# Sliding-window attention and a softplus feed-forward network: a fourth G buffer, two third differences in place, and the order of all steps rewritten

## The chip, the cores and the metric

The kernel runs on one core of one Trainium2 chip. Its time is the device time of one execution in microseconds (us); the figure for the kernel before is the median of three runs. Besides those runs there is one profiled execution, taken by the hardware profiler, with a time of its own. In profile rows PE is TensorE (PEld its weight loads), DVE is VectorE, ACT is ScalarE, POOL is GpSimd and SP is SyncE. POOL issues the loads, SP the DMA transposes and the stores.

## What is computed

The input is q, k, v of 4 batches, 8 heads, 768 positions and 64 columns, and two weight matrices, w_in (512 x 2048) and w_out (2048 x 512). Each position attends to the 8 first positions of its batch and to the 96 last ones up to itself, with a bias by distance whose slope depends on the head. The attention rows, 3072 tokens of 512 numbers, go through a feed-forward network with a softplus between its two products.

```python
rel = pos[:, None] - pos[None, :]
is_global = pos[None, :] < n_global                 # 8
is_local = (rel >= 0) & (rel < n_local)             # 96
dist = np.where(is_global & ~is_local, n_local, np.abs(rel))
scores = q @ k.T / sqrt(D) - slopes * dist          # else -1e9
a = softmax(scores)
x = (a @ v).transpose(0, 2, 1, 3).reshape(3072, 512)
h = x @ w_in
g = np.maximum(h, 0.0) + np.log1p(np.exp(-np.abs(h)))
return g @ w_out
```

## The kernel before

The tokens are cut into 24 blocks of 128 (six for each batch) for the attention, and into 12 chunks of 256 (two blocks each) for the network. A chunk's result of the softplus, with 2048 rows in 16 pieces of 128 x 256, is the tile G.

The program is a list of 1139 steps, the string ORDER (line 748). A step is a kind, one or two indices, and at the end for some kinds a digit that says which engine does it (0 DVE, 1 ACT; for the small copies gk and gv, 2 is POOL). Each engine carries out its instructions in the order of this list, so that the list alone sets every engine's order and that of the DMA queues. An instruction waits for the data that it reads and for the readers of the memory that it overwrites; everything behind it on its engine waits with it. The kinds:

- `lq`, `lk`, `lv` load q, k or v of a block, `wi` and `wo` parts of the weights (L103, L109, L114). All are issued by POOL, one after another. The rings for q and k hold six blocks in three tiles of a pair each, the ring for v seven. In the profile `k_t` stands for any tile of K's ring; in the order below `k_t2_83` is the tile of blocks 16 and 17, among others, and `k_t0_81` that of block 19.
- `t`, `tQ`, `tK` transpose q and k of the first blocks on PE, and `qc`, `kc` copy them to QT and KT. From block 8 on, `d` transposes q and k by DMA, issued by SP (L270, L271).
- `gk` and `gv` copy the eight global keys or values of the batch into a block's tiles (L312, L316). The copy of values goes into the tile of the block before, once that has been read for its own product.
- `s`, `ss` are the scores (L325), whose matmuls use half the array's rows; `ab`, `ac` add the bias (DVE, L385 and L394); `e` is the Exp (ACT, L405), which writes the weights Pb; `p` is the value product (PE, L421), half a block at a time; `nm` divides by the sum (DVE, L436 and L439) and writes the attention rows xsf. For the first blocks the bias is put into PSUM by a matmul instead (`z`, L351).
- `x` transposes attention rows on PE (L454) and `xc` copies them (L461) into XT; in later blocks `y` does it by DMA from SP.
- `f`, `fe`, `lp`, `o`, `os` are the plain network of the first chunks (L475 to L640).
- From chunk 2 on the first product is made by seven smaller products of a Strassen type: `ht` differences of x (DVE, L553), `h` the products (PE, L582), `hc` copies of one accumulator (ACT or DVE, L592, L595), `hv` sums of two (DVE, L607; the operand is called p_ps), `he` Exp (ACT, L612), `hl` the logarithm into G (ACT, L616). They use sums of quarters of w_in, made once by `hw` (DVE).
- From chunk 1 on the second product is made in the same manner: `gs` sums of G (DVE, L668), `m` the products (PE, L698), `ec` and `ev` evictions (L727 on ACT or DVE, L737 on DVE), `st` the stores (L711). They use differences of parts of w_out, made once by `wd` (DVE, L653).
- `g` is a gate (POOL, L746): a copy of one element of G, by which POOL waits there until ACT has written that part of G, so that the loads behind it do not start sooner.

The accumulators take turns in three banks of PSUM by the string BANKS (line 206); the scores and value products have banks of their own. G has three buffers.

```python
ffn = ctx.enter_context(tc.tile_pool(name="ffn", bufs=3))             # G
w_dif = {i: const.tile([P, NU, CT], F16, name=f"w_dif{i}") for i in (1, 2, 3, 4)}
def gv(n, by=0):
    if n % BPB >= 2:
        engine_copy(by)(v_t[n - 1][0:NG], v_t[first_of(n)][0:NG])
def gate(s):
    c, u = divmod(s, NU)
    nc.gpsimd.tensor_copy(gate_t[:], G[c][0:1, 2 * u + 1, 0:1])
for name in ORDER.split():
    kind = name.rstrip("0123456789.")
    KINDS[kind](*(int(i) for i in name[len(kind) :].split(".")))
```

The functions that the change touches:

Of the kernel before, what the change touches and what calls it, by code (L numbers as in the profile page):

```python
# [13 lines left out]
F16 = mybir.dt.float16  # L14
# [6 lines left out]
def kernel(  # L21
# [19 lines left out]
    CT = 2 * P  # L41
# [23 lines left out]
    ffn = ctx.enter_context(tc.tile_pool(name="ffn", bufs=3))  # L65
# [19 lines left out]
    w_dif = {i: const.tile([P, NU, CT], F16, name=f"w_dif{i}") for i in (1, 2, 3, 4)}  # L85
# [111 lines left out]
    def bias_part(half, part):  # L197
# [8 lines left out]
        "01201220102102102102012010010211021221212022020121202201001202012121011020020112"  # L206
        "022021102002111020202121010212020101"
# [285 lines left out]
    def plus(c, w):  # L493
# [146 lines left out]
    def w_half(i, j, part):  # L640
        return w_out_c[2 * i + part][:, :, CT * j : CT * j + CT]

    def w_dif_part(i, part, by=0):

        rows = slice(4 * part, 4 * part + 4)
        t = {n: w_dif[n][:, rows, :] for n in w_dif}
        a, b = {
            1: (w_half(0, 1, part), w_half(0, 0, part)),
            2: (w_half(1, 1, part), t[1]),
            3: (w_half(1, 1, part), w_half(0, 1, part)),  # L650
            4: (w_half(1, 0, part), t[2]),
        }[i]
        sum_by(by)(t[i], a, b, ALU.subtract)  # L653
# [5 lines left out]
    def g_sum(c, i, by=0):  # L659
# [21 lines left out]
        7: lambda c: (SM[c, 3], lambda k: w_dif[3][:, k, :]),  # L681
# [61 lines left out]
    def gate(s):  # L743
# [5 lines left out]
        lq1 bb0.1 w18 lk1 cq0 ck0 tq0 z0.0 z0.1 lq2 lk2 bb1.1 tk0 bb1.0 s0.1 lv0 t1 s0.0 lv1  # L749
        kc1.0 e0.1 lk4 z1.1 bb0.0 qc1.0 s1.1 e0.0 tQ2 e1.1 z1.0 s1.0 z2.1 tK2 lv2 gv19 p0.1 e1.0  # L750
        gk2.1 p0.0 qc2.0 lq4 lv3 kc2.1 nm0.1 nm0.0 wi1 z2.0 wi3 s2.0 s2.1 x0 lk5 qc3.1 kc3.0
        p1.0 gk3.2 p1.1 e2.0 nm1.0 z3.0 lq5 e2.1 s3.0 gv2.2 wi0 lv4 p2.0 wi2 p2.1 wi4 xc0.1
        nm1.1 z3.1 s3.1 e3.0 nm2.0 gv3.0 nm2.1 x1 t4 x2 e3.1 wo0 xc1.0 qc4.1 gk4.1 p3.0 p3.1
        kc4.1 nm3.0 nm3.1 f1 s4.0 lv5 xc2.1 wi6 fe1 x3 xc3.1 f3 f9 fe3 ab4.0 fe9 s4.1 wo1 t5
        ab4.1 qc5.0 wo2 f11 kc5.0 gk5.0 e4.0 f0 gv4.1 f8 wo3 e4.1 fe0 fe11 p4.0 nm4.0 lp0 s5.0
        fe8 f2 p4.1 ab5.0 fe2 nm4.1 f10 s5.1 gv5.1 f5 lk6 lq6 fe10 e5.0 lk7 lp1 x4 f4 ab5.1
        xc4.0 hw1.0 e5.1 lq7 wd1.0 f12 o0 p5.0 fe12 fe4 lp4 f13 fe13 o4 lq8 hw2.0 nm5.0 p5.1
        hw3.1 fe5 nm5.1 lp5 f14 hw4.0 fe14 lv6 hw1.1 lk9 f7 lp2 f6 x5 lk8 lq9 lv7 xc5.1 fe7 o1
        fe6 o5 lp3 f15 lq10 h2.1.0 fe15 hc2.1.0.1 o2 hw2.1 ht2.1 ht2.3 lp6 lp7 wd1.1 lk10 h2.5.0
        h2.2.0 gs1.3 hc2.5.0.1 hw3.0 wd3.0 wd2.0 ht2.2 wd2.1 ht2.4 wd4.1 o6 h2.6.0 d8 o7  # L760
        he2.11.0 wd3.1 t6 os0.1.1 hv2.6.0 kc6.1 h2.3.0 o3 gs1.1 hw4.1 qc6.1 gs1.2 he2.12.0
        os0.0.1 ss6 ab6.0 h2.7.0 ac6.1 t7 e6.0 kc7.1 hv2.7.0 lq14 d9 ac6.0 hl2.0.0 m1.1.0 st0.0
        qc7.0 p6.0 ec1.1.0 e6.1 h2.4.0 nm6.0 ss7 gk8.2 he2.22.0 he2.21.0 lv8 ac7.0 h2.1.1
        hc2.1.1.1 p6.1 ab7.0 m1.6 ac7.1 d10 ec1.6.1 lk11 e7.0 h2.5.1 wd4.0 h2.2.1 nm6.1 h2.6.1
        hc2.5.1.1 m1.2.1 g7 p7.0 hv2.6.1 he2.11.1 nm7.0 x6 e7.1 xc6.1 hl2.1.0 ev1.2 h2.7.1
        h2.3.1 hv2.7.1 lq11 p7.1 ss8 g15 nm7.1 ab8.0 he2.12.1 m1.7 ac8.0 x7 gk9.2 he2.22.1 ac8.1
        ec1.7.1 h2.4.1 xc7.1 ht3.1 m1.4 gs1.4 ss9 e8.0 ec1.4.0 lq13 h3.1.0 gv8.2 p8.0 he2.21.1
        e8.1 hc3.1.0.1 m1.5.0 ac9.0 nm8.0 lv10 h3.5.0 h3.2.0 ht3.3 ht3.2 lv9 lq12 hl2.1.1 h3.6.0
        ev1.5 m1.3 p8.1 hc3.5.0.1 lv11 d11 ab9.0 he3.11.0 hl2.0.1 h3.1.1 hv3.6.0 h3.7.0 h3.3.0
        ht3.4 ev1.3 nm8.1 st1.0 e9.0 hv3.7.0 he3.12.0 gs2.1 gv9.2 ac9.1 y8 m2.1.0 hc3.1.1.1  # L770
        h3.4.0 p9.0 h3.2.1 ec2.1.0 gk10.1 gs2.2 nm9.0 he3.21.0 e9.1 gs2.3 g21 st0.1 he3.11.1
        h3.6.1 h3.5.1 lk12 hc3.5.1.1 p9.1 hl3.0.0 nm9.1 hv3.6.1 ss10 m2.6 y9 gv10.2 ab10.0
        h3.3.1 he3.22.0 h3.7.1 gk11.2 ec2.6.1 ac10.0 m2.7 lq17 hv3.7.1 h4.1.0 he3.12.1 ac10.1
        lk15 e10.0 hl3.0.1 ec2.7.1 p10.0 nm10.0 lq16 h3.4.1 ht4.1 ss11 he3.21.1 m2.4 lk13 ac11.1
        e10.1 ac11.0 d12 ht4.2 ec2.4.1 ht4.3 h4.5.0 hc4.1.0.1 g27 hc4.5.0.1 ab11.0 lk14 m2.2.1
        h4.6.0 hl3.1.0 hv4.6.0 p10.1 e11.0 d13 h4.2.0 m2.5.0 h4.7.0 nm10.1 g23 st1.1 y10 gv11.2
        p11.0 he4.11.0 gs2.4 ev2.5 ev2.2 nm11.0 h4.3.0 e11.1 g13 m2.3 ht4.4 hv4.7.0 he3.22.1
        ss12 p11.1 ev2.3 h4.4.0 he4.12.0 hl3.1.1 he4.21.0 lv16 ac12.0 h4.1.1 ab12.0 lv12
        hc4.1.1.1 h4.5.1 m3.1.0 gs3.1 hc4.5.1.1 ec3.1.1 nm11.1 gs3.2 lq15 h4.6.1 ac12.1 y11
        hv4.6.1 he4.22.0 gs3.3 h4.2.1 gs3.4 m3.6 e12.0 he4.11.1 gk12 g11 h4.7.1 lk19 e12.1  # L780
# [132 lines left out]
```

## Time and profile before

| | us |
|---|---|
| median of 3 runs | 200.42 (200.15 to 200.73) |
| the profiled execution | 200.62 |
| its span, first to last instruction | 198.68 (the page rounds to 198.7) |
| PE busy | 191.9 (97% of the span) |
| ACT busy | 176.8 (89%) |
| DVE busy | 172.6 (87%) |
| POOL busy | 82.2 (41%) |

The span is what lies between the first and the last instruction of the core; the time is longer by 1.94 us, which lie around it. Busy times of PE overlap, since matmuls are pipelined; what PE is kept from is read from the distances between the starts of its instructions. The granted clock of PE is 1.000 throughout. In a row of the timeline the first two numbers are the start and the duration in us, then come engine, line, operation and tiles, and in brackets the idle time of that engine ahead of the row, with what ended it. In the grouped rows the numbers behind the bar are busy us, mean ns of one, and idle us ahead of them.

### The profile page before, as it was taken

To read this page: it belongs to the slowest core of one execution; us is meant where nothing else is said; L and a number is where in the kernel's file an instruction comes from. 1 tells how busy PE (TensorE), PEld (TensorE's weight loads), DVE (VectorE), ACT (ScalarE), POOL (GpSimd) and SP (SyncE) were. 2 spreads that over 40 slices of the span, in tenths; PEclk is the share of its full clock that TensorE was granted. 3 is DMA by queue.
4 is the path that set the end of the run, shared out by engine and by line. 5 is a ranking of instruction groups with operands and counts; after the bars stand their busy time and mean duration, and the time that the engine had idled before them with its cause. 6 is when DMAs were issued, how large, how long until landed. Compare 5 with 4: busy or idle time off the path is not lost.

```text
span 198.7 us, 6702 instructions
## 1 busy us (share of the span) xinstructions
PE 191.9 (97%) x2743; PEld 167.1 (84%) x2745; DVE 172.6 (87%) x400; ACT 176.8 (89%) x285; POOL 82.2 (41%) x136
## 2 busy tenths in 40 slices
PE   7799999999999999999999999999999999999993
PEld 2457887768989889999988999999898999999993
DVE  7567587899999989999989999999999999876662
ACT  2989899999999999999998999999999999988600
POOL 8989733380595467384034968211040020000000
PEclk9999999999999999999999999999999999999999
DMA  7999999999999999999997999996692411401314
GB/s 126 160 162 180 196 198 206 194 155 151 168 156 149 202 137 123 166 132 187 146 129 160 151 153 157 133 130 101 77 160 45 135 28 30 158 3 37 127 55 156
DMA packets 108542, 26.91 MB, mean 135 GB/s; under 512 B 99552, under 2 KB 106208, under 8 KB 108512
## 3 DMA queue, kind: packets, MB, share of 16 engines
q0 software_dynamic: 76000, 13.37, 91.6%
q1 hardware_dynamic: 31472, 12.85, 37.1%
q8 instruction: 21, 0.34, 0.7%
q10 hardware_dynamic: 1040, 0.26, 0.6%
q14 instruction: 9, 0.07, 0.1%
HBM read 27.26 MB, written 6.29 MB: 169 GB/s over the span
## 4 chain that ended last, share of the span: by engine, by line
PE 53%; DVE 30%; DMA 10%; issue 3%; POOL 2%; ACT 0%; DVEq 0%; POOLq 0%
PE o L698 19%; PE hT L582 10%; PE hT L475 7%; DMA k_t<-in_k_dram 5%; DVE Z L394 5%; PE p_ps L582 4%; DVE sum L668 4%; DVE xsf L439 4%; DVE Z L385 3%; PE o L627 3%; DMA KT<-k_t 3%; DVE p_ps L607 3%; PE x_ps L421 2%; DMA XT<-xsf 2%; DVE e_sb L607 2%
## 5 line engine op out<-in xcount | busy, mean ns | idle before, releaser
L616 ACT ACTIVATE G<-e_sb 128x1024 f16<-128x1024 f32 x40 | 42.4, 1069 | 0.2
L582 PEld LDWEIGHTS <-w_sum 128*128 128x128 f16 x640 | 39.3, 98 | 2.8 <-issue 1.1
L405 ACT ACTIVATE Pb<-Z 128x1024 bf16<-128x1024 f32 (+1 forms) x40 | 39.8, 1001 | 0.9 <-DVE Z L385 0.5
L698 PEld LDWEIGHTS <-sum 128*128 128x128 f16 x352 | 32.7, 98 | 3.7
L698 PE MATMUL o<-w_dif,sum 128*128 128x256 f16 x264 | 34.1, 273 | 0.0
L582 PEld LDWEIGHTS <-w_in 128*128 128x128 f16 x480 | 29.1, 98 | 0.8
L698 PEld LDWEIGHTS <-G 128*128 128x128 f16 x272 | 24.8, 98 | 2.8
L582 PE MATMUL hT<-x_dif,w_sum 128*128 128x128 f16 x320 | 24.4, 219 | 0.7 <-DVE p_ps L607 0.6
L385 DVE TENSOR_TENSOR Z<-s_ps,biasA 128x1024 f32<-128x1024 f32 x19 | 23.1, 1217 | 2.0 <-PE s_ps L325 2.0
L582 PE MATMUL hT<-XT,w_in 128*128 128x128 f16 x320 | 24.4, 219 | 0.0
L612 ACT ACTIVATE e_sb<-hT 128x512 f32<-128x512 f32 x40 | 23.9, 604 | 0.1
L316 POOL COPY v_t<-v_t 8x520 bf16<-8x520 bf16 x12 | 7.3, 608 | 40.4 <-PE x_ps L421 40.4
L103 POOL DMA_DIRECT2D q_t<-in_q_dram x21 | 18.8, 894 | 11.9 <-PE hT L582 7.0
L103 POOL DMA_DIRECT2D k_t<-in_k_dram x21 | 18.7, 896 | 9.2 <-DMA w_out<-in_moe_w_out_dram 5.3
L103 POOL DMA_DIRECT2D v_t<-in_v_dram x24 | 21.3, 891 | 2.0 <-DMA w_out<-in_moe_w_out_dram 1.6
L698 PE MATMUL o<-w_out,G 128*128 128x256 f16 x168 | 21.8, 273 | 0.0
L439 DVE TENSOR_TENSOR xsf<-x_ps,rcp 128x256 f16<-128x256 f32 x44 | 18.7, 424 | 1.5
L421 PE MATMUL x_ps<-v_t,Pb 128*128 128x65 bf16 x324 | 17.2, 193 | 0.1
L421 PEld LDWEIGHTS <-Pb 128*128 128x128 bf16 x352 | 15.3, 97 | 1.7 <-ACT Pb L405 0.2
L475 PE MATMUL hT<-XT,w_in 128*128 128x256 f16 x128 | 15.6, 273 | 0.0
L668 DVE TENSOR_TENSOR sum<-G 128x1024 f16<-128x1024 f16 x22 | 15.4, 702 | 0.0
L325 PEld LDWEIGHTS <-KT 64*128 64x128 bf16 x352 | 10.0, 94 | 6.3 <-issue 2.3
(124 smaller groups left out, 386.1 us busy)
## 6 DMA issues: line engine op xcount, KB each, us to landing
out_dram<-osb SPq DMA_DIRECT2D x18, 256.0 KB, 3.7
v_t<-in_v_dram POOLq DMA_DIRECT2D x24, 128.0 KB, 6.2
q_t<-in_q_dram POOLq DMA_DIRECT2D x21, 128.0 KB, 6.1
k_t<-in_k_dram POOLq DMA_DIRECT2D x21, 128.0 KB, 6.3
w_out<-in_moe_w_out_dram POOLq DMA_DIRECT2D x4, 512.0 KB, 14.9
out_dram<-osb SPq DMA_DIRECT2D x10, 128.0 KB, 2.1
w_in<-in_moe_w_in_dram POOLq DMA_DIRECT2D x4, 256.0 KB, 7.1
w_in<-in_moe_w_in_dram POOLq DMA_DIRECT2D x2, 512.0 KB, 10.8
```

Source lines behind the costliest of these rows:

```text
L103: nc.gpsimd.dma_start(dst[n][:, :, 0:D], src[b, :, i * P : (i + 1) * P, :].rearrange("h s d -> s h d"))
L325: nc.tensor.matmul(dst(4 * sub + 2 * mm + t), KT[n - t][rows, m, :], QT[n][rows, m, :], start=not pre and not (whole and (t or mm)), stop= ...
L385: nc.vector.tensor_tensor(Z[:], buf[:, 0:8, :], biasA[:, half, :, :], ALU.add)
L405: nc.scalar.activation(Pb[:, 0:nreg, :], src, AF.Exp, scale=inv_sqrt)
L421: nc.tensor.matmul(x_b[:, lh, :], Pb[:, r, :], v_t[n - t][:, h, :], start=(t == 0), stop=(t == 1 or first),)
L439: nc.vector.tensor_tensor(xsf[:, h0 : h0 + 4, :], x_b[:, :, 0:D], rcp[:, h0 : h0 + 4][:, :, None].to_broadcast([P, 4, D]), ALU.mult,)
L475: nc.tensor.matmul(hT[:, j, :], w[:, m, fo : fo + P], XT[c][:, m, :], start=(j == 0 and m == 0), stop=(m == KM - 1), skip_group_check=(j > 0),
L582: nc.tensor.matmul(o[:, b, :], lhs(k, b), rhs[:, k, :], start=(i in (1, 5) and b == 0 and k == 0), stop=(k == KH - 1), skip_group_check=True,)
L612: nc.scalar.activation(o, t, AF.Exp)
L616: nc.scalar.activation(g_tile(c)[:, b0 : b0 + HB, :], HS.pop((c, i, u))[:], AF.Ln, bias=1.0)
L668: sum_by(by)(SM[c, i][:], a(), b(), op)
L698: nc.tensor.matmul(o, lhs[:, k, :], rhs(k)[:, c0:c1], start=(i in (1, 2, 5) and k == 0), stop=(k == NU - 1), skip_group_check=(i not in (1 ...
```

## The change

It does four things.

1. The pool of G has four buffers.
2. The third difference of w_out has no tile of its own. It is written over the upper right quarter of w_out, one of its two operands, which no product reads any more once the plain products of the first chunk have been made. Product 7 reads it there.
3. The third sum for w_in likewise is written over the rows 0 to KH of the w_in tiles 4 and 6, one of its operands.
4. ORDER and BANKS are new. The 1139 steps are the same; their places differ, and for some copies the engine's digit. By digit: the copies of K go from three on DVE and four on ACT to seven on DVE, those of Q from four and three to five and two, those of attention rows from two and six to three and five; evictions go from 18 on DVE and 26 on ACT to 15 and 29, copies of an accumulator of the first product from six and 34 to five and 35. Four small copies of global keys go from ACT to DVE, and one of values each from DVE and from ACT to POOL.

```diff
-    ffn = ctx.enter_context(tc.tile_pool(name="ffn", bufs=3))
+    ffn = ctx.enter_context(tc.tile_pool(name="ffn", bufs=4))
...
-    w_dif = {i: const.tile([P, NU, CT], F16, name=f"w_dif{i}") for i in (1, 2, 3, 4)}
+    w_dif = {i: const.tile([P, NU, CT], F16, name=f"w_dif{i}") for i in (1, 2, 4)}
...
     w_sum = {
-        (i, u): const.tile([P, KH, HB * P], F16, name=f"w_sum{i}_{u}") for i in (1, 2, 3, 4) for u in (0, 1)
+        (i, u): const.tile([P, KH, HB * P], F16, name=f"w_sum{i}_{u}") for i in (1, 2, 4) for u in (0, 1)
     }
+    w_sum.update({(3, u): w_in_c[4 + 2 * u][:, 0:KH, :] for u in (0, 1)})
...
         t = {n: w_dif[n][:, rows, :] for n in w_dif}
+        t[3] = w_half(0, 1, part)
...
-        7: lambda c: (SM[c, 3], lambda k: w_dif[3][:, k, :]),
+        7: lambda c: (SM[c, 3], w_block(0, 1)),
...
     ORDER = """
...
-        he4.22.1 lq18 p12.1 h4.4.1 ac13.1 lv14 ec3.7.1 ht5.1 he4.21.1 d15 lk17 lk16 ac13.0
+        ev2.3 lq16 lk16 gv11.2 nm10.1 h4.7.0 h4.3.0 hv4.7.0 p11.0 he4.12.0 y10 e11.1 gs3.3 ss12
...
```

The first place is DVE near the start, where the attention rows of block 2 are normalised (L436, L439) and the first XT is copied (L461). A number behind an underscore tells buffers apart. Before:

```order
L436 RECIPROCAL rcp_418<-x_ps_145 128x4
L439 TENSOR_TENSOR xsf_417<-x_ps_145,rcp_418 128x256
L316 COPY v_t2_86<-v_t0_84 8x520
L436 RECIPROCAL rcp_418<-x_b_392 128x4
L439 TENSOR_TENSOR xsf_417<-x_b_392,rcp_418 128x256
L461 COPY XT_332<-tr_x_424 128x4x128
```

and with the change:

```order
L461 COPY XT_342<-tr_x_343 128x4x128
L436 RECIPROCAL rcp_407<-x_b_385 128x4
L439 TENSOR_TENSOR xsf_406<-x_b_385,rcp_407 128x256
L436 RECIPROCAL rcp_407<-x_ps_144 128x4
L439 TENSOR_TENSOR xsf_406<-x_ps_144,rcp_407 128x256
L260 COPY KT_437<-tr_420 128x512
```

The copy of global values (L316) is no longer in DVE's queue there; a copy of XT stands ahead of the two halves of the block's rows, and the halves have changed places.

The second place is POOL's queue at the load of K of block 16 (tile `k_t2_83`). Before, K of 17 and K of 16 are the pair `x2`, behind the loads of q of block 18 and v of block 14:

```order
L103 DMA v_t6_90<-in_v_dram 128x8x64
L312 COPY KT_1682<-KT_1626 128x4x8
L103 DMA q_t0_78<-in_q_dram 128x8x64
L103 DMA v_t0_84<-in_v_dram 128x8x64
L103 DMA k_t2_83<-in_k_dram 128x8x64 x2
L746 CAST gate_t_158<-G_985 1x1
L103 DMA v_t1_85<-in_v_dram 128x8x64
```

With the change:

```order
L103 DMA v_t4_88<-in_v_dram 128x8x64
L748 CAST gate_t_155<-G_1488 1x1
L103 DMA q_t2_80<-in_q_dram 128x8x64
L103 DMA k_t2_83<-in_k_dram 128x8x64
L316 COPY v_t3_87<-v_t6_90 8x520
L103 DMA q_t0_78<-in_q_dram 128x8x64
```

K of 16 now stands ahead of the copy of values for block 11 (into `v_t3_87`), 69 steps of the list earlier; K of 17 is no longer beside it.

The third place is POOL's queue at the load of K of block 19 (tile `k_t0_81`). Before:

```order
L103 DMA v_t2_86<-in_v_dram 128x8x64
L103 DMA v_t5_89<-in_v_dram 128x8x64
L103 DMA q_t1_79<-in_q_dram 128x8x64
L746 CAST gate_t_158<-G_721 1x1
L103 DMA k_t0_81<-in_k_dram 128x8x64
L103 DMA v_t6_90<-in_v_dram 128x8x64
```

With the change:

```order
L316 COPY v_t1_85<-v_t5_89 8x520
L103 DMA v_t6_90<-in_v_dram 128x8x64
L103 DMA k_t2_83<-in_k_dram 128x8x64
L748 CAST gate_t_155<-G_2239 1x1
L103 DMA v_t3_87<-in_v_dram 128x8x64
L103 DMA k_t0_81<-in_k_dram 128x8x64
L748 CAST gate_t_155<-G_1488 1x1 x2
```

It has moved from step 478 of the list to step 681, behind the copy of values of block 16 (into `v_t1_85`) and the loads of v of block 20, K of block 22 and v of block 17; behind it stand gates.

More of the change, by code (lines that the diff above doesn't have):

```diff
@@ L755 @@
[L755 to L760, printed above, removed]
@@ new lines @@
+        s3.1 nm2.0 t4 x2 lq5 gv3.2 kc4.0 gk4.2 qc4.0 xc1.1 p3.0 e3.1 p3.1 s4.0 wi0 xc2.1 lv4 f1
+        nm3.0 wi2 nm3.1 ab4.0 x3 f3 wi4 s4.1 xc3.1 fe1 f9 fe3 e4.0 wo0 lv5 t5 fe9 ab4.1 gv4.1
+        f11 qc5.0 kc5.0 f8 fe11 f0 e4.1 wi6 p4.0 gk5.2 s5.0 wo1 f10 nm4.0 fe0 lp0 fe10 f2 ab5.0
+        wo2 s5.1 fe8 wo3 ab5.1 p4.1 hw1.0 f5 e5.0 fe2 lq6 nm4.1 f4 fe5 gv5.2 lq7 f12 f13 o4 lp1
+        lp5 hw2.0 lk6 lk7 lq8 lk8 fe12 wd1.0 hw3.0 o0 hw4.0 lv6 p5.0 lp4 lq9 fe4 gs1.3 gv12
+        hw1.1 x4 lk9 f15 fe13 e5.1 nm5.0 f6 xc4.1 hw2.1 p5.1 nm5.1 wd1.1 fe15 f7 fe6 f14 lp2 o5
```

162 lines of the change are left out of this document (81 added, 81 removed).

## Prediction

> **What bounds the kernel now.** I read the page first (the span, the busy times), then the windows of busy time, then the chain of waits, then PE's rows in order of time.
>
> ```profile
> span 198.7 us, 6702 instructions
> PE 191.9 (97%) x2743; PEld 167.1 (84%) x2745; DVE 172.6 (87%) x400; ACT 176.8 (89%) x285; POOL 82.2 (41%) x136
> ```
>
> ```profile
> 10.00:20.00 10.00, 9.50 (x165) 6.69 (x167) 7.04 (x21) 9.17 (x16) 9.38 (x14) 1.00 2.05 171
> 50.00:60.00 10.00, 10.00 (x165) 9.06 (x163) 9.86 (x24) 10.00 (x18) 8.22 (x14) 1.00 2.20 161
> 180.00:190.00 10.00, 10.00 (x118) 9.25 (x116) 6.61 (x14) 6.83 (x10) 0.00 (x0) 1.00 0.24 81
> ```
>
> The columns are stretch, length, then busy us (and instructions) of PE, PEld, DVE, ACT and POOL, then granted clock and DMA. PE is full; in the middle DVE and ACT are full beside it (9.86 and 10.00 of 10), and at the end they are not (6.61, 6.83). A busy PE can still be waiting, since a matmul's tail overlaps the next, so the pace is read from start to start:
>
> ```profile
> 163.43 0.24 PE x_ps L421 x8
> 178.95 0.45 PE p_ps L582 x8
> 179.40 0.87 PE o L698 x8
> ```
>
> Eight 128-column matmuls take 0.45 us, eight of 256 columns 0.87, eight value products 0.24, each group following the last without a hole. Where PE keeps these distances it can't be sped up by any order. The change leaves PE's work as it is, so it can only remove holes. From 17 to 160 us the view of waits has two groups for PE, this and one of 0.3 us on a transposed K, whose row stands further below:
>
> ```profile
> PE hT L582 <- DVE p_ps L607: 0.6, 2, 0.5
> ```
>
> (us in total, times, longest). What of the span is not matmul pace lies in the start, in the change of array shape at each score group, in the tail, and in a few holes. Those named below come to 1.25 us (0.28, 0.34, 0.63); with some too small for the view of waits I estimate 2 us that an order could close.
>
> **The change part by part.** The sum is made against the profiled execution, 200.62 us, whose span is 198.68; the 1.94 around it stays. It lies 0.2 above the median of 200.42, so I take the sum off the median.
>
> *The new buffers and the in-place differences: 0.* The third w_out difference and third w_in sum remain the same instructions of the same width, written elsewhere:
>
> ```profile
> L616 ACT ACTIVATE G<-e_sb 128x1024 f16<-128x1024 f32 x40 | 42.4, 1069 | 0.2
> ```
>
> Each must now wait for PE's last reader of the block that it overwrites: `hw3.0` stands behind `f12` and `f13`, `hw3.1` behind `f7` and `f14`, `wd3.0` behind `o0` and `o4`, `wd3.1` behind `o1`. All readers stand earlier in the list; behind a late one DVE's queue would hold its x differences and the next score additions. The G row's last number is ACT's idle time before 40 writes of G: 0.2 us, so nobody waits for a third G and a fourth frees no one. Its worth is the order that it allows.
>
> *The start: -0.35.* PE's rows, with one of DVE:
>
> ```profile
> 12.53 0.39 PE L325 MATMUL oo<-QT,KT 64*128 64x128 bf16 x8
> 13.10 0.40 PE L454 MATMUL tr_x<-ident_h,xsf 128*128 128x128 f16 x4 [0.18 <-DVE xsf L439]
> 14.73 0.57 PE L421 MATMUL x_ps<-v_t,Pb 128*128 128x65 bf16 x8
> 15.14 0.41 PE L421 MATMUL x_b<-v_t,Pb 128*128 128x65 bf16 x8
> 15.90 0.68 DVE L316 COPY v_t<-v_t 8x520 bf16<-8x520 bf16 x1
> 16.69 0.39 PE L241 MATMUL tr<-ident,k_t 128*128 128x128 bf16 x4
> 17.18 0.40 PE L454 MATMUL tr_x<-ident_h,xsf 128*128 128x128 f16 x4
> 18.87 0.40 PE L325 MATMUL s_ps<-QT,KT 64*128 64x128 bf16 x8
> 19.20 0.40 PE L454 MATMUL tr_x<-ident_h,xsf 128*128 128x128 f16 x4
> ```
>
> Scores followed by transposes without a wait cost 0.33 (18.87 to 19.20); from 12.53 it took 0.57, a hole of 0.24. `p1.0` (0.24) now stands in that hole. The value product at 14.73 took 0.41 instead of 0.24 (hole 0.17): it waited for POOL's copy of the global values, which now stands ahead of a q load. Four transposes after 16.69 should take 0.23 and took 0.49 (hole 0.26), waiting for DVE, which had the 0.68 us copy of 15.90 in its queue; that copy goes to POOL. Together 0.67. Against it, `p3.1` follows sooner on the Exp that makes its weights, and I estimate a new wait of 0.3 there. Bounds -0.67 and 0; I take -0.35.
>
> *K of block 16: -0.97.* The one large hole in the middle:
>
> ```profile
> 87.81 10.20 DMA k_t<-in_k_dram
> ```
>
> ```profile
> 102.73 0.41 PE L421 MATMUL x_ps<-v_t,Pb 128*128 128x65 bf16 x8
> 103.41 0.40 PE L325 MATMUL s_ps<-QT,KT 64*128 64x128 bf16 x8 [0.27 <-DMA KT<-k_t]
> 103.81 0.53 DVE L553 TENSOR_TENSOR x_dif<-XT 128x256 f16<-128x256 f16 x2 [0.85 <-DMA XT<-xsf]
> 106.61 0.41 PE L421 MATMUL x_ps<-v_t,Pb 128*128 128x65 bf16 x8
> 107.48 0.61 PE L582 MATMUL hT<-x_dif,w_sum 128*128 128x128 f16 x8 [0.47 <-DVE p_ps L607]
> 122.57 0.41 PE L421 MATMUL x_ps<-v_t,Pb 128*128 128x65 bf16 x8
> 122.91 0.40 PE L325 MATMUL s_ps<-QT,KT 64*128 64x128 bf16 x8
> ```
>
> POOL issues the load at 87.81, it lands at 98.01, and PE's scores wait for SP's transpose of it until 103.41. SP is in order, so the transpose of attention rows behind it was late too, and DVE idled 0.85 us for it. PE lost 0.68 - 0.34 = 0.34 at 103.4 (0.34 is the same pair undisturbed, 122.57 to 122.91) and 0.87 - 0.24 = 0.63 at 107.48, where DVE's sum came late. In the new order the load stands ahead of the value copy of block 11, which ran at 75.2:
>
> ```profile
> 75.22 0.61 POOL L316 COPY v_t<-v_t 8x520 bf16<-8x520 bf16 x1 [2.11 <-PE x_ps L421]
> ```
>
> That is 12 us earlier; even 10.2 us of load lands by 86. What SP waits for next is K of block 17, issued there about where 16 was less one load, and needed 5 us later. Bounds -0.97 and 0 (if DVE, full anyway, gives the time back); I take all of it.
>
> *Copies moved between ACT and DVE: 0.* By the steps' engine digits, ACT loses five Q/K copies (592 ns), an XT copy, four small key copies and one of values, and gains three evictions and one h copy; DVE the reverse but for one value copy, which went to POOL.
>
> ```profile
> L727 ACT COPY u<-o 128x256 f32<-128x256 f32 x7 | 2.7, 387 | 0.9 <-PE o L698 0.9
> L595 ACT COPY hp<-p_ps 128x512 f32<-128x512 f32 x15 | 8.9, 592 | 0.4 <-PE p_ps L582 0.3
> L727 DVE COPY u<-o 128x256 f32<-128x256 f32 x4 | 1.7, 424 | 1.1 <-PE o L698 0.9
> L595 DVE COPY hp<-p_ps 128x512 f32<-128x512 f32 x5 | 3.4, 685 | 0.0
> L253 DVE COPY QT<-tr 128x512 bf16<-128x512 bf16 x4 | 1.7, 414 | 0.0
> ```
>
> DVE: six copies at 0.41, three evictions fewer at 0.42, one h copy fewer at 0.69, small ones +0.2: about +0.7 us. ACT: six at 0.59 and about 1.4 of small ones fewer, three at 0.39 and one at 0.59 more: about -3.2. Most of DVE's extra lies before 50 us, where the window 10 to 20 has 3 us of DVE idle to hide it; without that cover it costs 0.7. The best case is the hole that ACT ends, -0.28:
>
> ```profile
> 65.77 0.61 PE L582 MATMUL p_ps<-x_dif,w_sum 128*128 128x128 f16 x8
> 66.50 0.40 PE L421 MATMUL x_ps<-v_t,Pb 128*128 128x65 bf16 x8
> ```
>
> (0.73 where 0.45 is due). I take 0, nearest to the idle that covers it.
>
> *K of block 19: +0.3.* This load now stands behind the value copy of block 16 and three loads:
>
> ```profile
> 107.05 0.61 POOL L316 COPY v_t<-v_t 8x520 bf16<-8x520 bf16 x1 [2.85 <-PE x_ps L421]
> 107.61 0.88 POOL L103 DMA_DIRECT2D k_t<-in_k_dram  x1
> k_t<-in_k_dram POOLq DMA_DIRECT2D x2, 128.0 KB, 7.6
> KT<-k_t SPq DMA_TRANSPOSE x2, 4.1
> KT<-k_t SPq DMA_TRANSPOSE x1, 7.5
> ```
>
> The DMA rows are those of the windows 109:112, 130:138 and 112:115. The copy starts at T = 107.05, when block 15's product is done. It takes 0.56, two loads 0.87 each, a gate 0.13, a load 0.87: K of 19 is issued at T + 3.3 = 110.35, where `lk21` was, whose kind took 7.6: landed at 117.95. SP has two 1.2 us transposes of block 22 and one of Q 19 ahead, so K's transpose starts near 118.5, and lands at 122.6 with 4.1, at 126.0 with 7.5. The scores of 19 are due at 122.91 (T + 15.86). Bounds 0 and +3.1; behind it POOL issues gates and no load for some us, so 4.1 is the nearer row, and I take +0.3 for a margin of 0.3.
>
> Sum: -0.35 - 0.97 + 0 + 0.3 = -1.0: 199.6 in the profiled execution, **199.4** as a median. The tail stays: the last five products and stores stand in the same order.
>
> **The rivals.**
>
> *DVE gives it back.* In the stretch 50 to 60 DVE is busy 9.86 of 10; once K of 16 is punctual, DVE itself may set the pace from 45 to 145, and the two holes were only where its lateness showed. For it: one of them ends on DVE. Against it: DVE idled 0.85 just before, so it had lost that time to the DMA. Then the start alone remains, -0.35: 200.1, no change.
>
> *K of 19 is late (the other side).* Price: K's transpose at 7.5 gives 126.0, a hole of 3.1 at block 19's scores, and 0.6 behind it as at 107.48; less the 1.3 won: +2.4, 202.8. It decides from a load and transpose together above 12 us; at 14 the gain is gone. For it: K of 16 took 10.20 in the same queue. Against it: nothing is issued behind it.
> The Trainium skill, "SBUF — State Buffer", section "SBUF: two separate sides", says that loads issued by GpSimd starve for descriptors while VectorE holds the port that the two share. By it a load could be late at any place where DVE is full, and the 10.20 would be no accident; with 10.20 in place of 7.6 the hole would be some 2.3 us. The row of 10.20 neither shows nor excludes that cause.
>
> *ACT's relief closes the rest.* The hole at 66.50 and the lesser ones go as well, since ACT is 10.00 of 10 there and loses 3.2 us: a further -0.28, and as much again for those too small for the view of waits: -1.6 with the start as forecast, 198.8, and 198.4 with the start's full 0.67. Against it: DVE is as full.
> The Trainium skill, "Perfetto Trace Analysis", section "Identifying the Most-Contended Engine", judges TensorE's room by the share of weight loads and not by matmul time. By it PE, at 84%, would have 16% free, ACT at 89% would be the tightest, and the 3.2 us might all be won. The trace differs: at 179 the groups stand at their shortest distances with the weight loads at 9.25 of 10, so 100% is not where PE fills.
>
> **How the numbers follow.** Forecast 0.47, DVE gives it back 0.25, K of 19 late 0.13, ACT's relief 0.15. A measurement of this kernel can't tell less than 0.3%, 0.6 us, from no change. Faster: 0.15, most of the forecast (0.40, the rest being a gain under 0.6), and 0.02 of the second: 0.57. Slower: 0.13, and 0.01 of the second: 0.14. Same: 0.29. The likeliest's own range is 198.9 to 199.9; to reach the second case, most of the last, and the early part of the late K (a hole of 1.8), the range is 198.3 to 200.9.
>
> **What would show it.** Start: the first ffn product after the third transposes starts 0.3 earlier against the work before it, and `x_ps` precedes `tr_x` after the second block's scores with no wait. K of 16: its load issued before 76, no wait on KT near 103, no DVE idle for XT there. K of 19: landing of its transpose against the scores of 19; a wait on DMA at PE near 122 means the late case. DVE's case: PE waits on p_ps, Z or xsf between 45 and 145 adding up to 1 us or more with no DMA behind them. The prediction is wrong if PE's holes after 17 us come to as much as before, or if a new load is waited for.

## The result, and the profile after

The changed kernel is slower by 0.6%: 201.74 us, the median of 22 runs (200.95 to 203.54), against 200.74 of 22 runs of the kernel before on the same chips (200.06 to 201.72). The ratio is 1.0061, with a 95% interval of 1.0042 to 1.0080. The forecast was 199.4, with a range of 198.3 to 200.9. The profiled execution of the change took 201.49 us, with a span of 199.48 at a granted clock of 1.0. Ratios below are to the kernel before, each with its 95% interval; they leave out executions more than 1.5% above the fastest of their kernel, three of six in the version below whose edits are the two loads and `p11.1`. In the changed file the lines around the ffn stand one or two lower than before (G is L617 instead of L616, the outer product L700 instead of L698).

The page's head, with the row of DMA share by slice; the last row is that of the page before, which the prediction had not shown:

```profile
span 199.5 us, 6712 instructions
PE 191.8 (96%) x2743; PEld 167.1 (84%) x2745; DVE 173.2 (87%) x405; ACT 174.2 (87%) x278; POOL 84.7 (42%) x138
DMA  8999999999999999999999994999621213201123
```

```profile
DMA  7999999999999999999997999996692411401314
```

PE's work is the same. ACT is 2.6 us shorter and DVE 0.6 longer, about as worked out (-3.2 and +0.7). The DMA row is what the prediction had overlooked: in both kernels the 16 DMA engines are 9 tenths busy or more in nearly every slice until about 135 us (a slice is 5 us). So a transfer that is issued sooner there may delay another; the experiments below bear on that.

PE's waits between 17 and 165 us, and ACT's between 60 and 100, in the changed kernel (us in total, times, longest):

```profile
PE x_ps L421 <- DMA v_t<-in_v_dram: 0.4, 1, 0.4
PE hT L583 <- ACT hT L593: 0.4, 1, 0.4
PE o L700 <- ACT osb L729: 0.4, 1, 0.4
PE hT L583 <- DVE p_ps L608: 0.3, 1, 0.3
PE p_ps L583 <- DVE x_dif L554: 0.2, 1, 0.2
```

```profile
ACT osb L729 <- DMA out_dram<-osb: 1.3, 1, 1.3
ACT hT L593 <- DVE Z L394: 0.7, 1, 0.7
```

No wait on K of 16 is left, and none on K of 19; five others have come. To price them I took every distance from the start of one group of matmuls to the next, less that group's own undisturbed distance, and added up by stretch. There are two profiled executions of the kernel before, the one of the prediction (span 198.68) and a second one of the same file (198.19):

| stretch, us | before | before, second | changed |
|---|---|---|---|
| 0 to 40 | 7.09 | 7.05 | 7.21 |
| 40 to 60 | 1.00 | 1.00 | 0.94 |
| 60 to 100 | 1.86 | 2.01 | 3.62 |
| 100 to 110 | 1.34 | 0.37 | 0.21 |
| 110 to 200 | 1.59 | 1.94 | 1.68 |
| sum | 12.88 | 12.37 | 13.66 |

Changed less second before is 1.29, which is the difference of the spans, and each column is one execution. The loss lies between 60 and 100 us (+1.61), a stretch to which the forecast gave nothing. Of the gain at 100 to 110, the -0.97 of the forecast, most is there in the second execution of the *unchanged* kernel too.

**The first new cause: a store.** The network's result of a chunk leaves from buffers called `osb`, a ring of two for each half of a chunk, so a chunk's half waits for the store of the same half two chunks back. ACT, SP and PE in order of time:

```profile
72.87 0.37 ACT L729 COPY osb<-o 128x256 f32<-128x256 f32 x1 [1.31 <-DMA out_dram<-osb]
```

```profile
66.66 0.53 SPq L713 DMA_DIRECT2D out_dram<-osb  x1
```

```profile
72.50 0.41 PE L421 MATMUL x_ps<-v_t,Pb 128*128 128x65 bf16 x8
73.29 1.03 PE L700 MATMUL o<-w_dif,sum 128*128 128x256 f16 x8 [0.38 <-ACT osb L729]
77.25 0.41 PE L421 MATMUL x_ps<-v_t,Pb 128*128 128x65 bf16 x8
77.92 0.61 PE L583 MATMUL hT<-x_dif,w_in 128*128 128x128 f16 x8 [0.27 <-DVE p_ps L608]
```

SP issues the store of chunk 0's second half at 66.66, it lands at 72.8, and ACT's copy of chunk 2, which writes that buffer again, has waited 1.31 us for it. PE's outer product needs the bank that the copy empties: 0.79 from 72.50 instead of 0.24, a hole of 0.54. ACT is then late: 0.43 at 77.5 (0.67 where 0.24 is due) and 0.31 at 78.8, which is 1.28 in all. The kernel before stored the same half 1.4 us earlier, against a copy at 73.02 where here it was due at 71.56:

```profile
65.30 0.58 SPq L711 DMA_DIRECT2D out_dram<-osb  x1
73.02 0.41 ACT L727 COPY osb<-o 128x256 f32<-128x256 f32 x1
```

In the list this store (`st0.1`) moved from step 362 to 390, directly ahead of the copy that needs its buffer.

**The second: a transpose that has too little work ahead of it.** From the chain of waits of the changed kernel, without its pieces of 0.06 us and less:

```profile
83.07 0.34 DVE xsf L439
83.53 5.58 DMA XT<-xsf
89.20 0.29 DVE x_dif L554
89.49 0.61 DVE Z L394
90.18 0.58 ACT hT L593
90.80 1.05 PE hT L583 x16
```

DVE normalises the rows of block 11, SP's transpose of them takes 5.58 us, and DVE's first x difference of chunk 5 waits 0.83 for it. The score addition behind it (Z) is late, then ACT's copy, then PE: holes of 0.15 at 89.4 and 0.55 at 90.2, 0.70 in all. (The 0.15 at 92.5 stands in the profiles without this wait too.) In the kernel before, PE's rows at the two ends, block 11's last value product and the first product that needs the transposed rows, are:

```profile
78.78 0.42 PE L421 MATMUL x_ps<-v_t,Pb 128*128 128x65 bf16 x8
88.33 0.61 PE L582 MATMUL p_ps<-x_dif,w_sum 128*128 128x128 f16 x8
```

That is 9.55 us of PE's work. With the change the two start at 81.61 and 89.54; less the hole of 0.15 that is 7.78. Normalising, transfer and difference take 1.9 + 5.6 + 0.3 = 7.8 here, without their waits: nothing is left over.

**The third, at the start:**

```profile
16.75 0.39 PE L454 MATMUL tr_x<-ident_h,xsf 128*128 128x128 f16 x4
17.53 0.40 PE L421 MATMUL x_ps<-v_t,Pb 128*128 128x65 bf16 x8 [0.40 <-DMA v_t<-in_v_dram]
```

0.78 where 0.23 is due: v of block 3 is now issued behind a block of w_in, and landed at 17.49, before at 15.53.

### The profile page after: what moved, and what is told of

It is laid out like the page before. It is cut to its first block, busy times and chain, and to the rows that moved or that the text cites. A ratio compares the mean times of both kernels' runs of the same rounds, so it can differ in the third digit from the quotient of the medians.

```text
span 199.5 us, 6712 instructions
## 1 busy us (share of the span) xinstructions
PE 191.8 (96%) x2743; PEld 167.1 (84%) x2745; DVE 173.2 (87%) x405; ACT 174.2 (87%) x278; POOL 84.7 (42%) x138
## 4 chain that ended last, share of the span: by engine, by line
PE 72%; DVE 12%; DMA 7%; POOL 4%; ACT 2%; issue 1%; DVEq 0%; POOLq 0%; ACTq 0%
PE o L700 27%; PE hT L583 17%; PE p_ps L583 7%; PE hT L475 7%; DMA v_t<-in_v_dram 4%; PE x_ps L421 4%; PE o L628 3%; PE s_ps L325 3%; DMA XT<-xsf 3%; DVE sum L670 3%; DVE Z L394 2%; DVE Z L385 2%; PE s_lo L325 1%; POOL v_t L103 1%; DVE xsf L439 1%; DVE p_ps L608 1%
## 5 line engine op out<-in xcount | busy, mean ns | idle before, releaser
L617 ACT ACTIVATE G<-e_sb 128x1024 f16<-128x1024 f32 x40 | 42.1, 1068 | 0.2
L583 PEld LDWEIGHTS <-w_in 128*128 128x128 f16 x640 | 39.0, 98 | 2.2 <-issue 1.0
L700 PEld LDWEIGHTS <-sum 128*128 128x128 f16 x352 | 32.8, 98 | 4.2 <-issue 0.5
L583 PEld LDWEIGHTS <-w_sum 128*128 128x128 f16 x480 | 29.2, 98 | 1.7 <-DVE x_dif L554 0.7
L316 POOL COPY v_t<-v_t 8x520 bf16<-8x520 bf16 x14 | 8.7, 623 | 43.7 <-PE x_ps L421 42.3
L700 PEld LDWEIGHTS <-G 128*128 128x128 f16 x272 | 24.9, 98 | 2.6
L583 PE MATMUL hT<-x_dif,w_in 128*128 128x128 f16 x320 | 24.4, 219 | 0.3 <-DVE p_ps L608 0.3
L700 PE MATMUL o<-w_dif,sum 128*128 128x256 f16 x176 | 22.8, 273 | 0.4 <-ACT osb L729 0.4
L700 PE MATMUL o<-w_out,sum 128*128 128x256 f16 x176 | 22.8, 273 | 0.0
L700 PE MATMUL o<-w_out,G 128*128 128x256 f16 x168 | 21.8, 273 | 0.0
L439 DVE TENSOR_TENSOR xsf<-x_ps,rcp 128x256 f16<-128x256 f32 x44 | 18.7, 424 | 1.5
L421 PE MATMUL x_ps<-v_t,Pb 128*128 128x65 bf16 x324 | 17.1, 193 | 0.5 <-DMA v_t<-in_v_dram 0.4
L608 DVE TENSOR_TENSOR p_ps<-hp,hT 128x512 f32<-128x512 f32 x20 | 13.8, 692 | 3.5 <-PE hT L583 2.7
```

What stands on the lines that cost most here:

```text
L421: nc.tensor.matmul(x_b[:, lh, :], Pb[:, r, :], v_t[n - t][:, h, :], start=(t == 0), stop=(t == 1 or first),)
L439: nc.vector.tensor_tensor(xsf[:, h0 : h0 + 4, :], x_b[:, :, 0:D], rcp[:, h0 : h0 + 4][:, :, None].to_broadcast([P, 4, D]), ALU.mult,)
L583: nc.tensor.matmul(o[:, b, :], lhs(k, b), rhs[:, k, :], start=(i in (1, 5) and b == 0 and k == 0), stop=(k == KH - 1), skip_group_check=True,)
L608: nc.vector.tensor_tensor(t, HS[c, "p", u][:], HT[c, "x", u][:], ALU.add)
L617: nc.scalar.activation(g_tile(c)[:, b0 : b0 + HB, :], HS.pop((c, i, u))[:], AF.Ln, bias=1.0)
L700: nc.tensor.matmul(o, lhs[:, k, :], rhs(k)[:, c0:c1], start=(i in (1, 2, 5) and k == 0), stop=(k == NU - 1), skip_group_check=(i not in (1 ...
```

## The experiments

The edits are made in the list of steps, which sets each engine's order; "..." stands for steps in between. Names: `st0.1` a store, `lv3`, `lk14`, `lq14` loads of v, k, q of a block, `wi1` a load of w_in, `y11` the transposes of block 11's rows, `ht5.1` an x difference of chunk 5, `ac13.0` the score addition of block 13, `gs8.3` a sum of G, `ec2.4.1` the copy into `osb`.

### One cause undone at a time

The two stores of chunk 0 sooner, in the changed kernel:

```diff
- x6 d9 lk12 ... p9.1 st0.0 gs2.3 ... g21 gs2.4 st0.1 ec2.4.1
+ x6 d9 st0.0 st0.1 lk12 ... p9.1 gs2.3 ... g21 gs2.4 ec2.4.1
```

> The new order with one edit: both stores of chunk 0 are issued right behind the DMA transposes of block 9, where SP is idle, and not behind those of blocks 10 and 11. Theory (a store lands too late): ACT's copy of product 4 of chunk 2 into osb waits 1.31 us for the second store to land at 72.79; PE's holes at 72.7 (0.54), 77.5 (0.43) and 78.8 (0.31) are that one wait and what it delays. All three go: -1.2 us against the changed kernel, equal to the kernel before within 0.3. Rival (the engines are too full in the new order, the store is only where it shows): the hole at 72.7 goes and at least as much of DVE or ACT waiting appears at 77 to 95: -0.5 at most, so still 0.5 us or more above the kernel before.

Measured: 1.0028 [0.9997, 1.0058], median 200.98. That is half of the loss; the interval overlaps that of the changed kernel, so by itself this run does not prove it. Whether the three holes went can't be read from it; they are gone in the version with v of block 3 as well, below.

V of block 3 ahead of the w_in load, in the changed kernel:

```diff
- z2.1 wi1 ... s2.0 lv3 e2.0
+ z2.1 lv3 wi1 ... s2.0 e2.0
```

> The new order with one edit: POOL issues the load of v of block 3 ahead of the first part of w_in, as in the kernel before. Theory (a load lands too late): v of block 3 lands at 17.49 in the changed kernel and at 15.53 before, and PE waits for it, a hole of 0.56 at 16.9. With the edit it lands before 16.5 and the hole goes: -0.5 us against the changed kernel, about +0.6 against the kernel before. Rival (the start is bound by the weights, which land later by the same edit): the first network products wait instead, 0.

1.0073 [1.0043, 1.0103]. The hole at 16.9 is gone in its profile, and the time is not better than the changed kernel's. In its place stands a hole of 0.27 at 17.1, where `p3.1` waits for its Exp, which ends at 17.30. That PE then meets the same late transfers a little sooner is my reading of the rest, and not shown.

The score addition ahead of the x difference, in the changed kernel:

```diff
- gv18 ht5.1 ac13.0 h4.4.1
+ gv18 ac13.0 ht5.1 h4.4.1
```

> The new order with one edit: DVE makes the second bias addition of block 13 ahead of the first x difference of chunk 5, not behind it. Theory (an instruction stands in the queue before its data): the difference waits 0.83 us for the DMA transpose of block 11, which lands at 89.10; the bias addition behind it holds ACT up for 0.70, and PE loses 0.55 at 90.2. With the edit DVE adds the bias at about 88.3 and that hole goes: -0.5 us against the changed kernel, about +0.6 against the kernel before. Rival (DVE is the bound from 45 to 145): the hole moves to the next sum, 0.

1.0053 [1.0027, 1.0079]: a miss. PE then waited for the x difference itself, 1.04 at 90.2, in a profiled execution in which the transpose was 1.1 us late and not 0.83. I read it so that the order on DVE decides only who hands the lateness of the transpose on.

Stores and v of block 3 together (the first two edits):

> The new order with two of the edits: both stores of chunk 0 behind the transposes of block 9, and v of block 3 ahead of w_in; the x difference of chunk 5 and the G sum of chunk 8 stay. Theory (a store lands too late, and what follows it): no ACT wait for a store near 72, no PE hole over 0.2 between 72 and 80, the hole of 0.35 at 160 stays. The hole near 90 tells whether it is a deadline of its own (it stays, 0.4 to 0.6) or a consequence of the store (it goes). Time: 1.7 us below the changed kernel, 0.5 us or more below the kernel before if the hole near 90 goes as well, else about equal to it. Rival (full engines): at or above the kernel before by 0.5, with DVE or ACT waits between 72 and 95.

1.0014 [0.9980, 1.0047]. The holes at 72 to 79 are gone, but in the profiled execution the transpose of block 11 was 2.1 us late for DVE, not 0.83. PE's waits from 17 to 165 us and DVE's from 60 to 100:

```profile
PE p_ps L583 <- DVE x_dif L554: 1.5, 2, 1.3
PE hT L583 <- ACT hT L593: 0.4, 1, 0.4
PE hT L475 <- DMA w_in<-in_moe_w_in_dram: 0.3, 1, 0.3
```

```profile
DVE x_dif L554 <- DMA XT<-xsf: 2.1, 1, 2.1
```

All four: those, the addition ahead of the x difference, and at 161 us the x difference of chunk 10 ahead of a sum of G (0.35 of hole there):

```diff
- p22.1 ab23.0 gs8.3 ht10.1 nm22.1
+ p22.1 ab23.0 ht10.1 gs8.3 nm22.1
```

> The three edits together, and a fourth: the third G sum of chunk 8 is made behind the first x difference of chunk 10, for which PE has a hole of 0.35 at 161.4. Theory (four late deadlines, independent of one another): -1.2 - 0.5 - 0.5 - 0.35 = -2.55 us against the changed kernel, 1.4 us below the kernel before. Rival (full engines): less than half of it, at or above the kernel before.

0.9979 [0.9942, 1.0016], median 200.11. Its interval lies wholly below that of the changed kernel: 1 - 0.9979 / 1.0061 = 0.8% faster, some 1.6 us of the 2.55 expected. So the loss is in these places of the order, and not in the new buffers. All that PE waited for from 17 to 165 us in its profiled execution, the fastest of its twelve (span 197.1):

```profile
PE s_ps L325 <- DMA KT<-k_t: 0.2, 1, 0.2
```

### Is the store's lateness an accident?

The changed kernel profiled a second time:

> The changed kernel once more, so that the others of this set have it on the same chip: 0.6% above the kernel before. Theory of the late store: a hole at 72 that ends on ACT's copy into osb, 0.3 to 1.5 us by how late the store lands.

1.0063 [1.0023, 1.0104], and the same wait (1.0 us) on a store that took 7.1. Then two loads of POOL (k and q of block 14) that are under way with it were issued later, the store left where the change has it:

```diff
- ht3.1 lk14 hc3.1.0.1 ... he3.12.0 lq14 gv9.2 ... g21 gs2.4 st0.1
+ ht3.1 hc3.1.0.1 ... he3.12.0 gv9.2 ... g21 lk14 lq14 gs2.4 st0.1
```

> The new order with one edit: k and q of block 14 are issued behind the gate at 67; the stores of chunk 0 stay where the new order has them. Theory (transfers queue): two loads of 0.85 us each leave the queue ahead of the late store, which lands 1 us or more sooner, and ACT's wait of 1.31 at 72 shrinks to 0.3 or less: -0.5 to -1.2 us against the changed kernel. Rival (the store is late since SP issues it late, whatever else is under way): it lands 6 us after its issue as before, 0.

The store's row in the view of DMA issues (queue, count, size, us to landing), of the changed kernel, of its second profile and of this one:

```profile
out_dram<-osb SPq DMA_DIRECT2D x1, 256.0 KB, 6.1
```

```profile
out_dram<-osb SPq DMA_DIRECT2D x1, 256.0 KB, 7.1
```

```profile
out_dram<-osb SPq DMA_DIRECT2D x1, 256.0 KB, 3.7
```

ACT's wait and the holes at 72 to 79 are gone. More profiles say the same: this store landed in 6.3 and 7.7 us in the versions with only v of block 3 or the score addition moved, in 4.2 in the last version of this section, which has the two loads later too, and in 3.7 and 4.1 in two executions of the kernel before. So what is under way beside the store changes its time, although another engine issues it. The Trainium skill, "DMA: Bandwidth & Descriptors", section "Issuing engines are not separate DMA queues", says that transfers of all issuers run interleaved on the same 16 engines; 6.1 and 7.1 against 3.7 agree.

Yet the time did not move: 1.0058 [1.0028, 1.0089]. PE's waits from 60 to 110 us, and DVE's row:

```profile
PE p_ps L583 <- DVE x_dif L554: 0.7, 1, 0.7
PE hT L583 <- ACT hT L593: 0.4, 1, 0.4
```

```profile
88.78 0.29 DVE L554 TENSOR_TENSOR x_dif<-XT 128x256 f16<-128x256 f16 x1 [1.56 <-DMA XT<-xsf]
```

PE arrives sooner at block 11's transpose, DVE's wait there grows from 0.83 to 1.56, and the gain is paid out there: 0.88 at 88.2 and 0.55 at 89.8.

The store late in the kernel *before*:

```diff
- g21 st0.1 he3.11.1 ... m2.6 y9 gv10.2
+ g21 he3.11.1 ... m2.6 y9 st0.1 gv10.2
```

> The kernel before with one edit: the second store of chunk 0 is issued behind the DMA transpose of block 9's attention rows, not ahead of it. By the trace of before it would then be issued at 69.75 and land at about 74.2, where ACT's copy into osb is due at 73.02. Theory (a store lands too late): ACT waits about 1.2 us there, and DVE and PE behind it lose 0.5 to 1.2 us: +0.8 against the kernel before. Rival (it is the new order's full engines that lose the time): ACT's wait is absorbed, within 0.3 of the kernel before.

1.0052 [1.0019, 1.0084]: this one step alone makes the old kernel slower by about as much as the whole change does. In the execution that was profiled, its fastest, the store took 3.7 us and landed at 73.16, the copy came at 73.49, and nobody waited. So the price shows in the times; that it is the wait which costs it here was not seen.

Last, the changed kernel with those two loads later and block 11's normalising and transposes ahead of other work (`p11.1` ahead of `m3.1.0`, `nm11.1` ahead of `gs3.2`, `y11` ahead of `d14`):

> The changed kernel with two of the edits alone: k and q of block 14 behind the gate, and block 11's value product, normalisation and transpose one place sooner. With the loads alone the late store's wait had gone (holes of 1.3 us between 72 and 79) and the time had not changed, since holes of 1.43 us stood at 88 to 90 where x differences waited for XT. Theory (the second transfer gave the gain back): both gone, 1.2 us below the changed kernel, 0.2 below or above the kernel before. Rival (DVE or ACT gives it back wherever it is won): 0.6% above the kernel before, as the loads alone.

1.0030 [0.9990, 1.0070]. Both holes are gone, and the next transfers are late. PE's waits from 60 to 110:

```profile
PE p_ps L583 <- DVE x_dif L554: 0.5, 1, 0.5
PE x_ps L421 <- DMA v_t<-in_v_dram: 0.3, 1, 0.3
PE hT L583 <- DVE p_ps L608: 0.2, 1, 0.2
```

The first is now at 103.9 (transposed rows for chunk 6), the second at 98 (v of block 15).

### What was K of block 16 worth?

The kernel before, profiled again:

> The kernel before once more, for a second profile of it. Theory (the 10.2 us that K of block 16 took to land was an accident of the one profiled execution): it lands in 7.5 us or less, no wait of PE for KT at 103, PE's two holes there (0.34 and 0.63) come to 0.4 or less together. Rival (it is always late there): 9 us or more, and the holes as before.

One run, 199.96 us, span 198.19. The loads of K of 17 and 16, one behind the other, and PE at the place of the old hole:

```profile
k_t<-in_k_dram POOLq DMA_DIRECT2D x2, 128.0 KB, 7.0
```

```profile
102.85 0.41 PE L421 MATMUL x_ps<-v_t,Pb 128*128 128x65 bf16 x8
103.19 0.40 PE L325 MATMUL s_ps<-QT,KT 64*128 64x128 bf16 x8
106.39 0.41 PE L421 MATMUL x_ps<-v_t,Pb 128*128 128x65 bf16 x8
106.64 0.61 PE L582 MATMUL hT<-x_dif,w_sum 128*128 128x128 f16 x8
```

0.34 and 0.25: no hole at either place. K of 16 took 7.4 us this time. In four profiled executions with that order of the load it took 10.2, 7.5, 7.4 and 6.8. The 10.2 is the exception among four and no property of the order. Without it the holes from 100 to 110 us were 0.97 less, but the span only 198.68 - 198.19 = 0.49 us. The Trainium skill, "DMA: Bandwidth & Descriptors", section "Anatomy of one DMA — SWDGE (gpsimd) path", gives 2.0 us and the bytes at 436 KB per us, an estimate of 2.3 us for these 128 KB; with the DMA engines 9 tenths busy the runs differ, and the measurement decides.

The load alone moved to the front in the kernel before, in two ways: exchanged with K of 19, and only a few steps ahead:

```diff
- h4.7.1 lk19 e12.1 ... d15 lk17 lk16 ac13.0
+ h4.7.1 lk16 e12.1 ... d15 lk17 lk19 ac13.0
```

> The kernel before with one edit: the loads of K of blocks 16 and 19 exchange their places in POOL's queue, so that K of 16 is issued some 8 us earlier and K of 19 is still early. Theory of the prediction (K of block 16 late costs 0.97): no wait for KT at 103, no DVE idle of 0.85 for XT, both holes (0.34 and 0.63) gone: -0.97 us against the kernel before. Rival (DVE gives it back, since it is the bound from 45 to 145): 0 to -0.3, with holes that end on DVE soon behind 103.

```diff
- ac13.1 lv14 ... d15 lk17 lk16 ac13.0
+ ac13.1 lk16 lv14 ... d15 lk17 ac13.0
```

> The kernel before with one edit: K of block 16 is issued ahead of v of block 14 and of K of block 17, so some 1.7 us sooner than before and not 9. Theory (an early load collides with the transposes of attention rows of blocks 10 and 11, issued from 78 to 82): here nothing is added to the transfers under way then, so no hole appears between 84 and 92, while K of 16 lands near 92 and the holes at 103 and 107 go: -0.9 us against the kernel before. Rival (DVE gives back whatever is won at 103): 0 to -0.3. Rival (each move of a load costs by chance, whatever its place): slower, as with K of 16 moved 9 us.

The exchange: 1.0045 [1.0011, 1.0078], slower. K of 19 had waited for its tile until 81.50 and so held the loads behind it back; K of 16 goes at 78.96, and the transposed rows of chunk 5 landed at 87.28 and 89.09 instead of 84.99 and 86.02. PE's waits from 80 to 110:

```profile
PE hT L582 <- DMA XT<-xsf: 0.7, 1, 0.7
PE p_ps L582 <- DVE Z L394: 0.4, 1, 0.4
PE o L698 <- DVE osb L737: 0.2, 1, 0.2
```

The second way: 0.9986 [0.9956, 1.0015], no gain that can be told. A gain of 0.97 (0.9952) lies just outside of this interval, one of half as much inside. So the step to which the forecast gave -0.97 was worth less than that, and nothing that can be told from zero; in the wrong place it cost.

### The buffers and the engine digits alone

The kernel before, with its order, and the new memory (four G, the third difference and sum in place; `hw3.1` had to move behind `hw3.0`):

> The order and the banks of the kernel before with the change's memory: four buffers for G, the third difference of w_out and the third sum of w_in in place; one step is moved, the second third sum of w_in, behind its last reader in the order of before. Theory (the new memory costs and wins nothing by itself; its waits are over when it is reached): within 0.3% of the kernel before. Rival (the in-place sum holds DVE up near 40, and the x differences behind it): 0.3% or more slower.

1.0005 [0.9973, 1.0037]: the memory costs nothing.

The changed kernel with the engines of 41 copies set back:

> The changed kernel with the engines of 41 copies between ACT and DVE set back to those of the kernel before (K, Q, XT, global keys, evictions, accumulators); the steps stand where the change has them, and copies to POOL stay. Theory (the four late transfers and orders make the change slower, the copies nothing): 0.6% above the kernel before, as the changed kernel. Rival (the copies moved to DVE, +0.7 us where it is full, are what makes the change slower): 0.3% or less above the kernel before. Rival (ACT's relief had won something): 0.9% or more above.

1.0524 [1.0468, 1.0579], 211.03 us. PE waits at many places; the first three rows of its waits over the whole span:

```profile
PE oo L421 <- ACT Pb L405: 1.6, 1, 1.6
PE o L700 <- DVE b L729: 0.8, 1, 0.8
PE s_ps L325 <- ACT QT L253: 0.8, 1, 0.8
```

By its letter this is the last rival's outcome, 0.9% or more, but 10 us are more than the 3.2 by which ACT was relieved. The order was laid for these digits: the run says that the two belong together, not what the digits are worth; that stays open.

### Versions meant to beat both

All four edits and `lq10` ahead of `lk11`:

> The new order with the four edits and a fifth: q of block 10 is loaded ahead of k of block 11, so that SP's transposes of blocks 10 and 11 start sooner. With the four edits K of block 11 landed at 70.85 and PE had a hole of 0.37 there. Theory (late deadlines): that hole goes, -0.3 us against the four edits, about 0.8 us below the kernel before in the median. Rival (DMA at that place is congested whatever the order): the transposes land no sooner, 0.

All four, k and q of 14 later, `lq19` behind `lv14`, and `wi6` ahead of `wo0`:

> The new order with the four edits and with loads set by when they are needed: k and q of block 14 (transposed at 80) are issued behind the gate at 67, not at 57 to 59; q of block 19 behind v of block 14; the last part of w_in ahead of the first of w_out. Theory (transfers queue in the 16 DMA engines, and a load issued early delays every transpose and store behind it): stores and transposes issued from 60 to 70 land in 4 to 5.5 us and not in 6 to 9.5, no PE hole over 0.3 that ends on a DMA between 30 and 95, and the single times lie closer together. 0.5 us below the kernel with the four edits, 0.9 below the kernel before. Rival (latency of 6 us and more is the transposes' own): landings as before, the same time as with the four edits.

The same without the move of `wi6`:

> The new order with both stores of chunk 0 early, v of block 3 first, the x difference behind the bias addition, the G sum of chunk 8 behind the x difference, k and q of block 14 behind the gate at 67, and q of block 19 behind v of block 14; w_in and w_out in the new order's places. In the set with w_in moved PE waited 1.02 us for w_out at 31. Theory: that hole goes and nothing else changes: 1.0 us below that set, 0.7 below the kernel before (ratio 0.9965). Rival (what is won is waited for at the next transfer): within 0.2% of the kernel before.

And with block 11's transposes sooner on top of it:

> The same, and the last value product of block 11, its normalisation and the DMA transpose of its rows each stand one place sooner on PE, DVE and SP (ahead of product 1 of chunk 3, of a G sum and of the transposes of block 14). Theory (PE's work between that value product and the first product that needs its rows, 7.8 us in the new order and 9.6 before, is too short for normalisation and a transfer of 5.5 to 6.8 us): the transfer starts 1.3 us sooner, and the wait of DVE for XT near 88 goes in every execution: 0.3 us below the same without it, and single times closer together. Rival (DVE is the bound there): equal or slower.

They gave 0.9979 [0.9948, 1.0010], 1.0013 [0.9982, 1.0043], 0.9985 [0.9956, 1.0014] and 1.0056 [1.0020, 1.0093]. In each profile something else was late: rows of block 8 (9.5 us for one transpose, 0.95 of hole at 71.7) and of block 11 (1.01 at 89), w_out at 31 (1.02), block 11's rows at 88 (0.77), v of block 15 and chunk 6's rows (0.63 and 0.77). Counting the four edits by themselves (0.9979), three versions lie 0.15 to 0.2% below the kernel before, each with 1 inside its interval. None can be called faster than it. The last version has no wait for block 11's rows left and is yet slower than the third, with intervals that do not meet: to remove the second cause alone was worth nothing here, since v of block 15 and chunk 6's rows were late instead.

## Why the prediction was wrong

**The step that failed is "K of block 16: -0.97 ... I take all of it."** It took one transfer's 10.2 us from one execution as a property of the order. Repeated, the same load took 6.8 to 7.5, and in the second profile of the kernel before the hole was not there; moved alone, the load gave 0.9986 [0.9956, 1.0015], no gain that can be told. So the path from load to hole was read rightly for that one execution, and the term's size was wrong: a median had nearly nothing to win there. In the changed kernel the load was issued at 77.66, a little after the 76 named as a sign, and nothing waited for it.

**What then made the kernel slower was in no term.** The prediction followed POOL's loads and looked at SP only for transposes and for the tail ("the last five products and stores stand in the same order"). It did not ask when a store in the middle frees its buffer, and did not price the work left between the rows of a block and their transposed use. Those two places are 1.28 and 0.70 us of the changed kernel's holes, and 0.35 stands at 161. Against them stand holes of the second profile of the kernel before that the new order did close: 0.36 at 66.2, 0.33 at 74.1, 0.36 at 109.9 and 0.32 at 139.1. The two sides leave 1.28 + 0.70 + 0.35 - 1.37 = 0.96 us. The two spans differ by 1.29, of which 0.16 lies ahead of 40 us; the medians differ by 1.0, and that the two agree so well is partly luck, since each profile is one execution. The runs show that the stores, v of block 3 and the order around the two x differences together hold the loss (0.9979 against 1.0061), and that a late second store alone makes the kernel before slower (1.0052). How it divides among them is read from the profile and only argued, since a gain at one place reappears at the next.

**The start, -0.35:** the three holes it named closed (0.17 to 0.26 each), but one of 0.23 opened at 13.6, and the wait for v of block 3 behind w_in, 0.56, was in no term. The Exp's wait, estimated at 0.3, shows as 0.27 once v is punctual. The stretch to 40 us became 0.12 to 0.16 longer. Undoing the wait for v alone brought no time that can be told.

**K of block 19, +0.3:** issued at 111.83, T + 3.3 as worked out with T = 108.53; landed in 6.0 us and transposed in 3.0 (bounds 7.6 and 4.1 to 7.5), ready before its scores at 123.78. The term is 0.

**The buffers, 0:** right. **The copies, 0:** the busy times changed as worked out, the worth could not be measured apart.

**The rivals.** "K of 19 is late" named the right kind of loss, a transfer that has too little time, at the wrong place; "ACT's relief" may be partly there, in the old holes that closed; its 198.4 should be 198.5 by its own terms. What makes single loads late, beyond what is under way beside them, no run here separates. The chance of 0.14 for slower came from one late load at one place. The DMA row of the page would have said that each transfer moved before 135 us could be the one.

## What to carry to other kernels

When steps are laid anew, work out for every transfer that is waited for (stores that free a ring's buffer as well as loads and transposes) how much work of the busiest engine now lies between its issue and its use, and compare that with how long its kind takes under load. A single long latency in one profile is no term of a sum until a second profile shows it again. Where the DMA row is full, expect that a transfer moved forward may make another one late, and that a hole closed ahead of a late transfer may come back at that transfer; both happened here.

## What the runs showed of the hardware

The landing time of one and the same transfer varied far more than the engines' times did: 6.8 to 10.2 us for a 128 KB load in the same order of issue, 3.7 to 7.7 for a 256 KB store, the longer ones with two more loads under way beside it. This was at a mean of 135 GB/s, with these packets:

```profile
DMA packets 108542, 26.91 MB, mean 135 GB/s; under 512 B 99552, under 2 KB 106208, under 8 KB 108512
```

92% of the packets are under 512 bytes, so the full DMA rows are full of small packets and not of bytes; that fewer, larger ones would ease it was not tried.
